# Block-diagonal factor built in head-innermost column order, plain copies of the folded weights, and a new written-out order

## The chip, the cores and the metric

The kernel runs on one core of one Trainium2 chip. The metric is device time in microseconds (us), the median of several runs. One more execution was taken by the hardware profiler; the rows quoted below come from it. Engine names are those of the profile: PE is TensorE (matmuls), PEld its weight loads, DVE is VectorE, ACT is ScalarE, POOL is GpSimd, SP is SyncE, whose queue issues nearly all DMAs.

## What is computed

A transformer block over 2048 tokens of width 512, batch 1. Its conditioning vector gives six vectors (shift, scale and gate, for each of two halves). The first half is linear attention with 32 heads of width 16, whose feature map is a small matrix per head and a softmax of both signs; the second half is a gated MLP of inner width 1376.

```python
h = _layernorm(x) * (1 + ca) + sa
qkv = h @ wqkv                                     # q, k, v: 32 heads of 16
pq = einsum('bhsd,hdf->bhsf', q, w_phi)            # the same for k
phi_q = concatenate([softmax(pq), softmax(-pq)])   # the same for phi_k
kv = einsum('bhsf,bhsd->bhfd', phi_k, v);  z = phi_k.sum(s)
o = (phi_q @ kv) / (phi_q @ z + 1e-6)
x = x + ga * (o @ wo)
h = _layernorm(x) * (1 + cb) + sb
x = x + gb * ((sigmoid(h @ w_gate) * (h @ w_up)) @ w_down)
```

All inputs are bf16. Note that `pq` is linear in `h`: `q` and `w_phi` can be folded into one 512 x 512 matrix per side, and so they are here.

## The kernel before

**Tasks and their order.** The kernel is a graph of 1230 named tasks. Each has a function that issues its instructions, the engines on which it may run with a planner's estimate of its cost in us, what it reads and writes, and the buffers that it uses. The string ORDER lists all tasks in one fixed sequence. A suffix (`@A`, `@D`, `@P`) puts a task on ACT, DVE or POOL; without it the first engine of its list is taken. Each engine executes its own tasks strictly in that sequence, and semaphores hold an instruction until its inputs are there. The position of a task against those of another engine says nothing by itself; its position against the tasks of its own engine, and which buffer slot it gets (there are eight PSUM banks), is what counts. The cost estimates are not read when the kernel is built: they only served to make the order.

**Names of tasks.** The digit or digits after a name are the token tile (128 tokens, 16 tiles), or a group of tiles and a quarter of the width:

- `ld_*` loads through SP: `x0b` tokens of tiles 2 and 3, `x0a` of tiles 0 and 1, `wk0/1` the two halves of the key weights, `wv0` the value weights, `wm00a..wm01b` four parts of the first modulation weights, `wmga` and `wmm2` the later ones (`wmm2` is 1536 KB), `wo`, `wg0`, `wu0`, `wd` the big weights.
- `warm*` matmuls on zeros whose result is not used; 6 in `warm0` and 12 `warm1_i`.
- `bd` (L578, POOL) builds the block-diagonal 128 x 128 matrices of `w_phi`, four of them, from `wp_sb` and a mask.
- `tpw`, `wTc` (L659, L662): key weights transposed on PE and copied to SBUF by ACT; `wqT` the same for the query weights by a DMA transpose.
- `fold1k` and `fold0k` (L677, PE): four 128-column matmuls each, transposed weights times `bd`; side 1 is the key side, side 0 the query side. `foldc1k` and `foldc0k` (L684 on ACT, L686 on DVE) copy the result from PSUM into `wqk_f`.
- `st1`, `rs1`, `nmr1`, `xn1`: LayerNorm of a tile; `tph` (L743) its PE transpose; `hm1_gj` (L750 on ACT, L752 on DVE and POOL) the modulation of quarter j of tile group g, which gives `h1T`. Groups 0 and 1 are tiles 0 and 1, group 2 is tiles 2 and 3, group 3 tiles 4 and 5, and so on. `modc1.h` (L628) and `modc1c h` (L633, L634) compute the vectors that `hm1` needs; `modca`, `modc2` (L614) compute later ones.
- `K`, `V`, `Q` (L816, L820, L870): the three projections of a tile, four 512-column matmuls each (an `a`/`b` pair is two halves). `e` and `qe` (L775, ACT) two exponentials of one PSUM bank; `n` and `qn` (L779, DVE) their sums; `r` the reciprocals; `phi` and `qphi` (L786, L783) the products; `va` (L835) the copy of V. `kv` (L282, PE) accumulates over tiles; `kvn`, `kvz` (L294, L299) end that accumulation in `kvb`.
- Behind `kvb`: `num`, `rd`, `u`, `oT`, `out`, `x1` (attention output), `st2`..`mod` (second LayerNorm), `g`, `tg`, `u`, `hm`, `y`, `fin`, `st` (the MLP and the store).

**Column order.** Within each group of 64 folded columns (4 heads of 16 features) everything behind the fold wants the head index innermost: column = feature x 4 + head. `bd` before has the feature innermost, as `w_phi` has. The order is changed in the copy from PSUM to SBUF:

```python
dst = wqk_f[:, kt_in, side * D:(side + 1) * D].rearrange("p (g f h) -> p g h f", f=DH, h=4)
src = ps[:].rearrange("p (g h f) -> p g h f", f=DH, h=4)
act.copy(dst, src)          # or dve.tensor_copy
```

so the source is read along the row and the destination is written at a step of four elements.

**Stages.** First, to about 16 us: loads, LayerNorm, transposes, the key-side fold. Then K and V of the first tiles and, from about 22 us, the query-side fold, without which no Q can run. From about 33 to 64 us: K, V, Q, exponentials, sums and products of all tiles, with `kv` accumulating. From 64 us on: attention output, second LayerNorm and MLP of each chunk of tiles, with the remaining Q tasks in between.

Of the kernel before, what the change touches and what calls it, by code (L numbers as in the profile page):

```python
# [39 lines left out]
ld_x0b wdz warm0 c1 warm1_0 warm1_1 warm1_2 warm1_3 warm1_4 warm1_5 warm1_6 warm1_7 bd ld_x1a st1_3 st1_2 st1_4 st1_5 ld_x0a ld_wk0 rs1_2 nmr1_2 rs1_3 tpw1  # L40
tpw0 wTc1 ld_x1b st1_1 wTc0 c2 xn1_2 xn1_3@A fold11 ld_wk1 rs1_1@P pmem ld_wm01b ld_wm01a st1_7 c3 ld_x2b foldc11 fold10 tpw3 foldc10 nmr1_3 warm1_8 tpw2
nmr1_1 wTc3 wTc2 modc1.1 st1_0 tph23 ld_wm00a ld_wm00b xn1_1 tph12 tph13 modc1c1 ld_x2a fold13 fold12 tph20 tph22 ld_x3a warm1_9 st1_6 xn1_4 rs1_0@P st1_11
st1_10 hm1_23@A hm1_13@A foldc13 xn1_0 hm1_12@A ld_wv0 wqT3 tph21 warm1_10 rs1_4@P modc1.0 foldc12@D nmr1_4 tph02 hm1_22@A xn1_5 modc1c0 rs1_6@P tph10 hm1_21
hm1_02@A hm1_20@A tph30 tph33 tph32 tph31 tph11 tph00 hm1_10@A st1_9 st1_8 nmr1_6 hm1_11@A hm1_00@A K2a hm1_30@A tph03 K2b tph01 e2.0 xn1_7 xn1_6 K3a hm1_32
hm1_33 hm1_01 K3b rs1_5@P K1a K1b ld_wmga wqT0 wqT1 wqT2 hm1_03 warm1_11 n2.0 tph42 tph41 K0a tph43 K0b e3.0 V2a V2b V1a xn1_10 hm1_42@A hm1_41@A nmr1_5
st1_15 xn1_8 xn1_11 st1_14 hm1_31@A e0.0 rs1_8@P hm1_43 tph40 V1b V3a xT1_11 xT1_10 n0.0 nmr1_8 fold03 fold01 va2 st1_12 fold00 V3b xn1_9 hm1_40 n3.0 e1.0
r0.0@A foldc01 foldc00 va1 foldc03 V5 fold02 foldc02 V0a V0b xn1_14 n1.0 tph52 hm1_52 xn1_15 va0 r3.0@A ld_wmm2 phi0.0 modca.0 tph82 Q1 modca.1 tph53 st1_13
ld_wo hm1_53 Q0 phi3.0@D r2.0@A phi2.0@D Q2 hm1_60@P r1.0@A hm1_82@A modcac hm1_63@P qe0.0 rs1_7@P nmr1_7 phi1.0@D xn1_13 qe1.0 qn0.0 qn1.0 qe2.0 va3 kv0.0
K4a K4b K6a V4 va4 qn2.0 tph51 kv1.0 e4.0 K6b kv2.0 tph50 K5a kv3.0 K5b xT1_13 hm1_62@P xn1_12 xT1_12 qphi0.0@P Q4 qphi0.1 hm1_50@A hm1_51@A V8 K7a e5.0 tph81
qe4.0 va5 K7b va8 hm1_73 V7 pT0 K8 qphi2.1 hm1_61@P qphi2.0@P n4.0 r4.0 tph80 n5.0 hm1_81 qn4.0 V6 phi4.0@D qphi1.0@P qphi1.1@P kv4.0 qphi4.0 hm1_71@P r5.0@A  # L50
va7 e6.0 hm1_80@A K10 tph83 qphi4.1 K9 va6 e7.0 pT2 n6.0 phi5.0 pT1 e8.0 hm1_83 r6.0 gwa n7.0 K14 n8.0 pT4 phi6.0 e9.0 K11 kv5.0 V10 gra ld_wd2 modc2.0 r7.0@A
n9.0 kv6.0 hm1_70@P hm1_72@P phi7.0@D e11.4 r8.0@A e11.6 e11.0 e14.4 phi8.0 modc2.1 modc2c e11.2 r9.0 n11.0 K13 kv7.0 V13 e10.0 e14.0 e13.0 e13.4 n11.4 n11.6
n14.4 n10.0 n11.2 r11.0 kv8.0 K12 phi9.0 V9 wmod_free gwb ld_wu0 ld_wg0 e12.0 K15 V11 r10.0@A va9 va10 va13 r11.6 n14.0 mask4 wo1 phi11.0 r11.4 r14.0 r11.2
n12.0 n13.0 kv9.0 r14.4@A e15.4 phi11.6@D Q6 V12 phi11.4 phi11.2 phi10.0@D e15.0 r12.0@A r13.0@A phi14.4@D phi14.0 Q3 kv10.0 n13.4 n15.4 V15 va11 kv11.0
kv11.2 kv11.4 V14 kv11.6 va12 phi13.0 qe6.0 r13.4 n15.0 r15.4 va15 phi15.4 phi13.4@D va14 Q5 ld_wd r15.0@A phi12.0@D kv12.0 kv13.4 kv14.4 kv13.0 kv15.4 qn6.0
qphi6.0@P qe3.0 phi15.0@D kv14.0 kv15.0 kvz1 kvn1 wo0 wo3 wo2 Q7 qphi6.1@P kvn0 kvz0 qn3.0 num1b num2b num0b num2a num0a qphi3.0@P num1a rd0a rd0b qe5.0 u0a
qe7.0 Q8 u0b grb num4b rd1b wo_all rd2a u1b rd1a rd2b u1a tpo0 oT0 u2b u2a oT2 pT6 qn5.0 Q11 num4a tpo1 oT1 out0 x1_0 qe11.0 out1 rd4a st2_0 x1_1 qphi3.1@P
qe8.0 pT3 Q9 wd0 Q15 Q13 rs2_0 nmr2_0 xn2_0 out2 xnT0 rd4b u4a u4b qn7.0 tsw Q10 mod02 mod03 mod00 x1_2 mod01@A qe15.0 g0.1 tg0.1 g0.8 st2_1 tg0.8 qphi5.1@P
qphi5.0@P u0.8 u0.1 g0.3 hm0.8 num3a hm0.1 g0.9 g0.6 u0.3 qe9.0 rd3a num3b qphi7.1@P qphi7.0@P tg0.3 tg0.9 u3a u0.9 hm0.3 rd3b hm0.9 u0.4 u0.6 u3b qe10.0
tg0.6 rs2_1 nmr2_1 u0.10 g0.4 hm0.6 num6a rd6a tg0.4 oT4 pT5 hm0.4 g0.10 g0.7 tg0.10 tg0.7 g0.0 u0.7 num6b g0.5 u6a xn2_1 hm0.7 hm0.10 tg0.0 qe13.0 tg0.5 wd8  # L60
wd3 wd1 wd5 rd6b u0.0 st2_2 out4 xnT1 mod12@A mod11@A mod10@A mod13@A Q12 oT3 pT7 out3 u0.5 u6b qn11.0 hm0.0 x1_4 g0.2 tg0.2 hm0.5 x1_3 g1.7 g1.5 oT6 u0.2
num7b u1.5 tg1.5 g1.0 wd4 hm0.2 rd7b hm1.5 qphi11.0@P u7b u1.0 u1.7 g1.1 num5b tg1.0 hm1.0 tg1.7 u1.1 hm1.7 st2_3 g1.3 u1.3 qphi11.1@P wd9 pT11 tg1.3 tg1.1
hm1.3 rd5b wd2 g1.4 u1.4 tg1.4 num5a num7a rd7a rd5a hm1.1 u7a out6 u1.6 g1.10 qe12.0 u5b tg1.10 u1.10 y0.0 g1.2 u5a x1_6 hm1.10 u1.2 oT7 rs2_2 nmr2_2 hm1.4
oT5 wd6 g1.6 tg1.6 Q14 y0.1 y0.2 g1.9 xn2_2 hm1.6 qn10.0 st2_4 xn2_3@D st2_6 xnT2 wd10 g1.8 num11a qphi10.0@P wd7 tg1.2 tg1.8 hm1.2 out7 out5 y0.3 tg1.9 x1_5
u1.8 y0.4 y1.0 qphi10.1@P y1.1 st2_5 hm1.8 y1.2 num11b y1.3 y1.4 u1.9 y0.5 y1.5 xnT3 mod22 rd11a y0.6 mod20@A mod21@A hm1.9 u11a rs2_3 pT10 mod23@P x1_7
nmr2_3 y1.6 y1.7 y1.8 y0.7 y1.9 y1.10 rd11b u11b fin1 g2.7 g2.5 u2.7 g2.0 u2.0 st2_7 tg2.5 xn2_5 tg2.7 hm2.7 qn9.0 tg2.0 qe14.0 rs2_4 hm2.0 xn2_4@P u2.5 g2.6
g2.1 tg2.1 nmr2_4 hm2.5 u2.1 hm2.1 g2.4 y0.8 g2.2 tg2.2 y0.9 tg2.4 qphi9.0@P xn2_6 u2.2 u2.4 num10b u2.8 u2.3 xn2_7 xnT5 xnT4 y0.10 g2.3 oT11 qphi9.1 hm2.4
qn8.0 mod32@P tg2.6 hm2.2 tg2.3 qn15.0 mod31@P qphi8.1@P qphi8.0@P qphi15.1@P mod33@P u2.6 y2.0 hm2.3 rd10b fin0 y2.1 y2.2 hm2.6 xnT6 pT9 g2.10 g2.8 tg2.8
tg2.10 out11 xnT7 pT8 mod43@A mod40@P u2.10 num10a g2.9 num9a mod42@A mod41@A x1_11 qphi15.0 y2.3 y2.4 y3.0 y3.1 y3.2 y2.5 u10b hm2.8 rd9a u9a rd10a u10a oT10
hm2.10 num9b rd9b u2.9 qn14.0 mod30@A tg2.9 y3.3 y3.4 y3.5 y3.6 y3.7 hm2.9 g3.0 qn13.0 qn12.0 u9b tg3.0 qphi12.1@P qphi12.0@P pT12 u3.0 hm3.0 g3.8 g3.3 num8a  # L70
tg3.3 rd8a tg3.8 st2_11 y3.8 u3.3 g3.1 u8a hm3.3 bnd3 u3.1 out10 x1_10 y3.9 y2.6 y3.10 y2.7 qphi13.1@P qphi14.1@P qphi14.0 u3.8 hm3.8 g3.7 g3.4 u3.7 y2.8
qphi13.0@P wr st1 tg3.1 bnd1 num12b st0 fin3 hm3.1 pT15 oT9 pT14 st2_10 tg3.7 tg3.4 y2.9 num8b g3.6 rd8b u8b num12a out9 y2.10 fin2 g3.2 u3.4 hm3.7 tg3.2
rs2_6 y4.0 y4.1 u3.2 hm3.4 nmr2_6 x1_9 hm3.2 xn2_10 xn2_11@P tg3.6 u3.6 g3.5 rd12b u12b u3.5 oT8 out8 num14b y7.0 tg3.5 hm3.6 st2_9 hm3.5 rd12a u12a x1_8
st2_8 num15a y5.0 rd15a u15a u3.9 y7.1 y5.1 y7.2 y7.3 num15b pT13 g3.9 rd15b u15b xnT10 st3 xnT11 oT15 st2 rs2_5 nmr2_5 xn2_9@P tg3.9 y7.4 y7.5 y4.2 y7.6 y7.7
hm3.9 rd14b g3.10 y4.3 u3.10 y5.2 xnT9 y5.3 y5.4 num13a mod62@A xn2_8 tg3.10 hm3.10 mod60@A out15 y4.4 y4.5 y7.8 num14a y6.0 xnT8 mod52@A x1_15 oT12 u14b
rd13a num13b y5.5 y5.6 y5.7 y5.8 y5.9 y5.10 fin5 rd13b mod61 y4.6 y6.1 y4.7 y4.8 y7.9 y6.2 out12 mod63 u13a mod50@P bnd2 y7.10 y4.9 u13b fin7 mod51@P mod53@A
u4.0 g4.0 u4.1 tg4.0 rd14a u14a oT14 hm4.0 g4.1 g4.5 tg4.5 u4.9 tg4.1 oT13 g4.2 out14 hm4.1 st2_15 x1_12 u4.5 y4.10 st7 y6.3 g4.8 tg4.8 u4.8 x1_14 hm4.5 bnd0
st2_14 fin4 st4 rs2_8 out13 x1_13 nmr2_8 g4.7 g4.6 tg4.7 g4.9 u4.7 st2_12 hm4.7 tg4.9 hm4.9 hm4.8 st2_13 y6.4 u4.4 y9.0 xn2_14@P xn2_15@P xnT15 xnT14 rs2_7
nmr2_7 y6.5 y6.6 y6.7 y6.8 u4.6 y6.9 u4.2 g4.4 tg4.2 st5 tg4.6 xn2_12@P xnT12 hm4.6 hm4.2 xn2_13@D xnT13 g4.10 u4.3 y8.0 y6.10 g4.3 tg4.4 y10.0 y9.1 mod83@A
tg4.3 mod81@A hm4.4 hm4.3 mod70 bndb y10.1 y8.1 u4.10 y9.2 y10.2 y8.2 y10.3 y8.3 y8.4 y8.5 y8.6 y8.7 y8.8 y11.0 mod71@P y10.4 y10.5 y10.6 y10.7 y10.8 y10.9  # L80
mod73@P tg4.10 mod82@P mod72@P mod80@A fin6 y9.3 y8.9 bndc y11.1 hm4.10 y8.10 y10.10 fin10 st10 fin8 g5.2 y9.4 g5.9 y9.5 y11.2 y9.6 u5.1 y9.7 y11.3 y11.4 y9.8
y9.9 tg5.2 u5.8 u5.2 hm5.2 g5.8 tg5.8 hm5.8 tg5.9 y11.5 y11.6 y9.10 u5.7 u5.0 g5.7 u5.5 st8 tg5.7 bndd hm5.7 st6 g5.3 g5.1 tg5.1 hm5.1 tg5.3 u5.3 g5.6 hm5.3
g5.0 tg5.0 hm5.0 u5.6 u5.9 tg5.6 g5.10 fin9 hm5.6 hm5.9 g5.4 y13.0 y13.1 tg5.4 tg5.10 u5.10 hm5.10 u5.4 y13.2 y11.7 g5.5 y13.3 y11.8 hm5.4 y11.9 y11.10 ldf
# [974 lines left out]
```

## Time and profile before

| what | value |
|---|---|
| median of 3 runs | 210.25 us (210.24 to 210.35) |
| the profiled execution's own time | 210.67 us |
| its span, first to last instruction | 208.8 us |
| around the span in that execution | 1.87 us |
| mean granted PE clock | 0.984 |
| last matmul ends (the last window with PE work) | 205.45 us |

The profiled execution is 0.42 us above the median. A table of windows gives, for each stretch, the us that each engine was busy, the number of instructions in brackets, the granted PE clock as a share of full speed, and the DMA share. A row of the groups gives line, engine, operation, output and inputs with shapes, count, total busy us, mean ns of one, idle time of the engine just ahead of them and what ended it. Instructions of one engine overlap a little at their ends, so group totals sum to more than the engine's busy time.

### The profile page before, as it was taken

The numbers are of one execution on the slowest core, as the hardware profiler recorded it, in microseconds if no ns is written. First come the engines' busy times: TensorE is split into PE (matmuls) and PEld (weight loads), VectorE is DVE, ScalarE is ACT, GpSimd is POOL, SyncE is SP. The second block draws the span as 40 slices with busy tenths as digits, with TensorE's granted clock in tenths as the row PEclk, the third lists the DMA queues.
The fourth block names the chain that finished last, engine by engine and source line by source line (L and its number), as shares of the span: only waits on it lengthen the run. The fifth ranks groups of instructions, "written<-read, shape, count | busy, mean of one in ns | idle before, by whom it ended". The sixth has DMA issues, their size and how long they took to land.

```text
span 208.8 us, 4136 instructions
## 1 busy us (share of the span) xinstructions
PE 198.0 (95%) x1448; PEld 107.7 (52%) x1471; DVE 162.5 (78%) x376; ACT 111.3 (53%) x257; POOL 101.8 (49%) x141
## 2 busy tenths in 40 slices
...
GB/s 179 332 318 182 62 358 81 109 122 56 279 394 167 126 80 102 68 87 53 87 139 28 100 127 85 69 101 25 75 0 72 57 27 25 52 6 25 6 52 79
DMA packets 49453, 22.94 MB, mean 110 GB/s; under 512 B 38065, under 2 KB 47634, under 8 KB 49426
## 3 DMA queue, kind: packets, MB, share of 16 engines
...
q14 instruction: 14, 0.11, 0.2%
q10 hardware_dynamic: 530, 0.02, 0.1%
HBM read 11.58 MB, written 2.10 MB: 66 GB/s over the span
## 4 chain that ended last, share of the span: by engine, by line
PE 70%; ACT 11%; DVE 8%; DMA 8%; issue 1%
PE y_ps L485 18%; PE u_ps L447 16%; PE g_ps L447 16%; DMA wmod_sb<-gdr 6%; PE k_ps L816 4%; PE a_ps L356 4%; ACT wqk_f L684 4%; PE q_ps L870 3%; ACT h1T L750 3%; PE v_ps L820 2%; ACT e L775 2%; DVE qks L779 2%; PE num L326 1%; DVE o L333 1%; DMA x_sb<-in_A_x_dram 1%
## 5 line engine op out<-in xcount | busy, mean ns | idle before, releaser
L457 ACT ACTIVATE tg<-g_ps 128x512 bf16<-128x512 f32 (+4 forms) x66 | 29.2, 456 | 70.3 <-PE g_ps L447 43.8
L468 DVE SCALAR_TENSOR_TENSOR wmod_sb<-tg,u_ps 128x512 bf16<-128x512 bf16 (+4 forms) x63 | 30.5, 492 | 18.6 <-ACT tg L457 12.2
L485 PE MATMUL y_ps<-wd_sb,wmod_sb 128*128 128x512 bf16 (+4 forms) x183 | 44.2, 366 | 0.2
L783 POOL TENSOR_TENSOR qphi<-qe,qks 128x512 bf16<-128x512 bf16 x25 | 26.3, 1070 | 9.2 <-issue 6.1
L447 PEld LDWEIGHTS <-wg_sb 128*128 128x128 bf16 (+1 forms) x252 | 21.6, 99 | 16.0 <-issue 0.4
L447 PEld LDWEIGHTS <-wu_sb 128*128 128x128 bf16 (+1 forms) x252 | 21.6, 99 | 15.7 <-issue 0.2
L485 PEld LDWEIGHTS <-wmod_sb 128*128 128x128 bf16 (+1 forms) x187 | 17.4, 98 | 17.8 <-issue 0.7
L447 PE MATMUL u_ps<-wT_sb,wu_sb 128*128 128x512 bf16 (+2 forms) x123 | 23.9, 322 | 0.1
L447 PE MATMUL g_ps<-wT_sb,wg_sb 128*128 128x512 bf16 (+2 forms) x120 | 23.4, 320 | 0.2
L447 PE MATMUL u_ps<-wqk_sb,wu_sb 128*128 128x256 bf16 (+4 forms) x128 | 19.9, 287 | 0.0
L447 PE MATMUL g_ps<-wqk_sb,wg_sb 128*128 128x128 bf16 (+4 forms) x127 | 19.6, 286 | 0.3
L779 DVE TENSOR_REDUCE qks<-qe 128x64 bf16<-128x1024 bf16 x16 | 19.1, 1207 | 0.4 <-ACT qe L775 0.4
L779 DVE TENSOR_REDUCE ks<-e 128x64 f32<-128x1024 bf16 (+2 forms) x22 | 19.2, 910 | 0.0
L492 DVE TENSOR_TENSOR ot<-y_ps,x 128x512 bf16<-128x512 f32 (+2 forms) x17 | 11.1, 652 | 10.4 <-PE y_ps L485 8.5
L870 PE MATMUL q_ps<-wqk_f,h1T 128*128 128x512 bf16 x62 | 17.3, 407 | 1.5 <-ACT wqk_f L684 1.4
L775 ACT ACTIVATE e<-k_ps 128x512 bf16<-128x512 f32 (+2 forms) x44 | 17.7, 521 | 0.1
L775 ACT ACTIVATE qe<-q_ps 128x512 bf16<-128x512 f32 x32 | 17.1, 612 | 1.0 <-PE q_ps L870 0.9
L786 POOL TENSOR_TENSOR phi<-e,kr 128x1024 bf16<-128x1024 bf16 (+2 forms) x11 | 15.2, 1391 | 4.9 <-ACT h1T L750 2.2
L816 PE MATMUL k_ps<-wqk_f,h1T 128*128 128x512 bf16 x61 | 15.9, 379 | 0.5 <-ACT h1T L750 0.3
L356 PE MATMUL a_ps<-wo_sb,oT 128*128 128x512 bf16 x60 | 15.9, 379 | 0.2
L820 PE MATMUL v_ps<-wv_sb,h1T 128*128 128x512 bf16 x61 | 15.9, 379 | 0.2
L376 POOL TENSOR_SCALAR ve<-mv 128x2 f32<-128x2 f32 (+1 forms) x8 | 1.8, 224 | 28.9 <-DVE mv L366 28.9
...
## 6 DMA issues: line engine op xcount, KB each, us to landing
...
wmod_sb<-in_w_mod_dram SPq DMA_DIRECT2D x1, 1536.0 KB, 7.1
wu_sb<-in_B_w_up_dram SPq DMA_DIRECT2D x1, 1376.0 KB, 7.6
wg_sb<-in_B_w_gate_dram SPq DMA_DIRECT2D x1, 1376.0 KB, 10.6
...
```

The costliest lines, as they stand in the source:

```text
L356: pe.matmul(ap_[:], lhsT=oT[:, j, :], rhs=wo_sb[:, j, :], start=(j == 0), stop=(j == KT - 1))
L447: pe.matmul(ps[:fsz, 0:n], lhsT=w[:, j, ft * P:ft * P + fsz], rhs=h[:, j, 0:n], start=(j == 0), stop=(j == KT - 1))
L457: G.add(f"tg{k}.{ft}", {"ACT": 0.13 + n * 0.00083}, lambda e, tg=tg, g_ps=g_ps, fsz=fsz, n=n: act.activation(tg[:fsz, 0:n], g_ps[:fsz, 0:n ...
L468: dve.scalar_tensor_tensor(hm_all[:fsz, hm[k].slot, ft, 0:n], tg[:fsz, 0:n], 1.0, u_ps[:fsz, 0:n], op0=ALU.add, op1=ALU.mult)
L485: mm = pe.matmul(y[:, 0:c1 - c0], lhsT=hm_all[:fsz, hm[k].slot, ft, tl * P:(tl + 1) * P], rhs=wd_sb[:fsz, ft, c0:c1], start=(ft == 0), sto ...
L775: act.activation(ee[:, a:b, s].rearrange("p g f h -> p g (f h)"), kp[:, a * 64:b * 64].rearrange("p (g n) -> p g n", n=64), ACT.Exp, scale ...
L779: dve.tensor_reduce(ks[:, a:b].rearrange("p g s h -> p (g s) h"), ee[:, a:b].rearrange("p g s f h -> p (g s) h f"), axis=AX.X, op=ALU.add)
L783: engine(e).tensor_tensor(ph[:].rearrange("p (g s f h) -> p g s f h", s=2, f=DH, h=4)[:, :, s], ee[:, :, s], ks[:, :, 1 - s].unsqueeze(2). ...
L786: engine(e).tensor_tensor(ph[:, a * P:b * P].rearrange("p (g f h) -> p g f h", f=DH, h=4), ee[:, a:b].rearrange("p g s f h -> p (g s) f h" ...
L816: pe.matmul(kp[:], lhsT=h1T[:, j, t * P:(t + 1) * P], rhs=wqk_f[:, j, D:2 * D], start=(j == 0), stop=(j == KT - 1))
L820: pe.matmul(vp[:], lhsT=h1T[:, j, t * P:(t + 1) * P], rhs=wv_sb[:, j, :], start=(j == 0), stop=(j == KT - 1))
L870: pe.matmul(qp[:], lhsT=h1T[:, j, t * P:(t + 1) * P], rhs=wqk_f[:, j, 0:D], start=(j == 0), stop=(j == KT - 1))
```

## The change

Three things are changed in one step.

1. `bd` is built with the head innermost, in two POOL instructions of half the width. They read `wp_sb` with each element repeated four times and the mask at a step of 16 elements.
2. The copies of the folded weights take the row as it stands; source and destination are both contiguous.
3. ORDER is replaced as a whole by another sequence of the same 1230 tasks. With it, the engine of 67 tasks changes; all eight `foldc` are on ACT. The task list also gains DVE as a permitted engine for the modulation of groups 6 and 7; no task of the new order uses it.

```diff
-    G.add("bd", {"POOL": 1.15}, lambda e: pool.tensor_tensor(
-        bd[:].rearrange("p k (h f) -> p k h f", f=DH), wp_sb[:].unsqueeze(2).to_broadcast([P, KT, 8, DH]),
-        bm.unsqueeze(1).to_broadcast([P, KT, 8, DH]), op=ALU.mult), w=["bd"])
+    def f_bd(e):
+        for g in range(2):
+            pool.tensor_tensor(bd[:, :, 64 * g:64 * g + 64].rearrange("p k (f h) -> p k f h", h=4), wp_sb[:].unsqueeze(3).to_broadcast([P, KT, DH, 4]),
+                               bm[:, 4 * g:4 * g + 4, 0].unsqueeze(1).unsqueeze(1).to_broadcast([P, KT, DH, 4]), op=ALU.mult)
+    G.add("bd", {"POOL": 1.25}, f_bd, w=["bd"])
...
-                dst = wqk_f[:, kt_in, side * D:(side + 1) * D].rearrange("p (g f h) -> p g h f", f=DH, h=4)
-                src = ps[:].rearrange("p (g h f) -> p g h f", f=DH, h=4)
+                dst = wqk_f[:, kt_in, side * D:(side + 1) * D]
                 if e == "ACT":
-                    act.copy(dst, src)
+                    act.copy(dst, ps[:])
                 else:
-                    dve.tensor_copy(dst, src)
+                    dve.tensor_copy(dst, ps[:])
...
-                w = {"ACT": 0.25 + 0.11 * n, "POOL": 0.12 + 0.165 * n}
+                w = {"ACT": 0.25 + 0.11 * n, "POOL": 0.12 + 0.165 * n, "DVE": 0.14 + 0.065 * n}
```

The head of the new ORDER, up to the first tiles' Q and a little beyond:

```
pmem ld_x0b wdz warm0 c1 warm1_0 warm1_1 bd st1_2 st1_3 warm1_2 warm1_3 c2 rs1_2 ld_x0a ld_wk0 warm1_4 tpw0 st1_0 rs1_0 wTc0 st1_1 ld_wk1 rs1_1 c3 xn1_0
nmr1_1 nmr1_2 ld_x1b st1_6 st1_7 tpw1 tpw3 wTc3 wTc1 tpw2 fold10 foldc10 wTc2 ld_wm00b ld_x1a ld_wm00a tph00 fold11 fold13 rs1_4 foldc13 fold12 foldc12 xn1_3
xn1_2 xn1_1 modc1.0 tph10 tph11 st1_4 tph20 tph01 ld_x2b foldc11 tph22 warm1_5 modc1c0 hm1_11@A nmr1_4 xn1_6 xn1_7 st1_5 rs1_3@P st1_11 st1_10 warm1_6
hm1_20@A hm1_10@A tph21 warm1_7 tph41 tph42 hm1_21 rs1_6@P nmr1_3 tph13 ld_wm01a ld_wm01b modc1.1 hm1_01@A hm1_00@A hm1_41@A tph03 tph23 K2a ld_x2a tph02
modc1c1 st1_8 ld_x3a warm1_8 K1a hm1_23 xn1_5 xn1_4 tph12 nmr1_6 st1_9 hm1_03@A hm1_13@A hm1_02@A ld_wv0 wqT3 xn1_10 xn1_11 rs1_5@P K0a K0b tph31 hm1_42@A
warm1_9 hm1_12@A hm1_22@A tph32 e0.0 K3a tph30 K3b hm1_30@A ld_wmga K1b tph33 warm1_10 tph40 st1_14 st1_15 st1_13 hm1_31@A hm1_32 wqT0 e3.0 wqT1 K2b hm1_40
nmr1_5 rs1_8@P n0.0 nmr1_8 hm1_33 e2.0 V0a V1a fold03 xn1_9 xn1_8 V1b V0b e1.0 n2.0 V2a V2b tph50 hm1_50 warm1_11 xn1_15 xn1_14 n1.0 V3a wqT2 fold00 fold01
tph43 r0.0@A va1 va0 phi0.0 foldc03 fold02 foldc01 foldc02 n3.0 st1_12 foldc00 xT1_10 xT1_11 r2.0 va2@D ld_wmm2 modca.0 modca.1 hm1_60@P hm1_63@P hm1_62@P
tph82 hm1_82@A r3.0@A modcac r1.0@A phi2.0@D phi1.0@D V3b K4a K4b rs1_7@P Q0 Q2 kv0.0 Q1 qe0.0 va3 qe2.0 hm1_43@A qe1.0 modc2.0 tph52 modc2.1 tph51 nmr1_7
xn1_12 xn1_13 phi3.0@D ld_wo qn0.0 modc2c e4.0 kv1.0 qn2.0 hm1_52 kv2.0 Q4 K5a kv3.0 xT1_12 xT1_13 qphi0.0@P
...
```

Of the tasks behind this head, the change moves `modc2.0`, `modc2.1` ahead (in the old order they stand behind `V10` and `K11`), moves `grb` (the broadcast load of the MLP's gate vector) ahead of `ld_wg0` and behind `ld_wd` and `ld_wu0`, and ends in the same tasks as before (`y15`, `fin15b`, `st15b`).

The matching stretch of the old ORDER, per engine: ACT has `rs1_2 rs1_3 wTc1 wTc0 c2 xn1_3 foldc11 foldc10 wTc3 wTc2 modc1c1 hm1_23 hm1_13 foldc13 hm1_12 hm1_22 modc1c0 hm1_02 hm1_20 hm1_10 hm1_11 hm1_00 hm1_30 e2.0 e3.0 hm1_42 hm1_41 hm1_31 e0.0 va2 e1.0 r0.0 foldc01 foldc00 va1 foldc03 foldc02`, with `foldc12` on DVE. SP has `ld_x0b ld_x1a ld_x0a ld_wk0 ld_x1b ld_wk1 ld_wm01b ld_wm01a ld_x2b ld_wm00a ld_wm00b ld_x2a ld_x3a ld_wv0 wqT3 ld_wmga wqT0 wqT1 wqT2 xT1_11 xT1_10 ld_wmm2 ld_wo`.

More of the change, by code (lines that the diff above doesn't have):

```diff
@@ L39 @@
 ORDER = """
[L40 to L83, printed above, removed]
```

41 lines of the change are left out of this document (38 added, 3 removed).

## The prediction

> **What bounds the kernel now.** I read the page first, then a table of windows, then the instruction groups of one stretch.
>
> ```profile
> PE 198.0 (95%) x1448; PEld 107.7 (52%) x1471; DVE 162.5 (78%) x376; ACT 111.3 (53%) x257; POOL 101.8 (49%) x141
> PE 70%; ACT 11%; DVE 8%; DMA 8%; issue 1%
> ```
>
> PE is busy for 95% of the span and holds 70% of the chain that ended last. ACT, 53% busy on average, still holds 11% of that chain, so there is a stretch in which ACT sets the pace. The windows show where (columns: length; busy us of PE, PEld, DVE, ACT, POOL; granted PE clock; DMA share).
>
> ```profile
> 5.33:26.20 20.87, 17.78 (x158) 10.66 (x159) 19.29 (x55) 19.75 (x44) 17.23 (x31) 0.92 1.00 223
> 26.20:34.00 7.80, 6.17 (x42) 3.03 (x43) 4.92 (x11) 6.74 (x17) 4.29 (x7) 0.78 0.70 264
> 34.00:63.70 29.70, 29.22 (x283) 16.37 (x287) 29.20 (x53) 29.15 (x83) 23.11 (x23) 1.00 0.66 188
> 63.70:100.00 36.30, 35.85 (x379) 24.58 (x381) 34.82 (x102) 23.34 (x59) 31.80 (x35) 1.00 0.44 90
> 100.00:205.45 105.45, 104.86 (x579) 51.66 (x588) 71.99 (x154) 31.04 (x58) 23.63 (x35) 1.00 0.28 59
> ```
>
> From 34 us to the last matmul PE loses 0.48 + 0.45 + 0.59 = 1.5 us in 171 us, so a reordering there can win 1.5 us at most. The loss is earlier. From 26.2 to 34 us PE is idle for 7.80 - 6.17 = 1.63 us and has a clock of 0.78, which loses another 0.22 x 7.80 = 1.7 us: **3.3 us together**. What PE waits for there:
>
> ```profile
> PE q_ps L870 <- ACT wqk_f L684: 1.4, 2, 0.9
> DVE h1T L752 <- PE tp_h L743: 2.5, 1, 2.5
> ```
> ```profile
> 26.57 2.41 ACT L684 CAST wqk_f<-fold_ps 128x512 bf16<-128x512 f32 x2
> 30.24 2.34 PE L870 MATMUL q_ps<-wqk_f,h1T 128*128 128x512 bf16 x5
> ```
>
> The first Q waits for the last copies of the query-side fold, which end at 26.57 + 2.41 = 28.98 us; PE runs without gaps only from 30 us on, and DVE stands 2.5 us behind a transpose that is queued on PE behind that Q. ACT is full up to there, and the copies are its largest group. ACT from its first LayerNorm instruction to the first `qe`:
>
> ```profile
> L684 ACT CAST wqk_f<-fold_ps 128x512 bf16<-128x512 f32 x7 | 8.6, 1342 | 0.0
> ...
> L750 ACT ACTIVATE h1T<-tp_h,modc 128x256 bf16<-128x256 bf16 x8 | 4.3, 563 | 0.0
> L750 ACT ACTIVATE h1T<-tp_h,modc 128x128 bf16<-128x128 bf16 x6 | 2.5, 456 | 0.0
> L662 ACT COPY wT_sb<-tp_w 128x512 bf16<-128x512 bf16 x4 | 2.2, 622 | 0.0
> ...
> L726 ACT ACTIVATE xn<-x_sb,nmr,rs 128x512 bf16<-128x512 bf16 x1 | 0.8, 821 | 0.0
> L775 ACT ACTIVATE qe<-q_ps 128x512 bf16<-128x512 f32 x1 | 0.6, 597 | 0.9 <-PE q_ps L870 0.9
> L708 ACT ACTIVATE ve<-mv,eps 128x2 f32<-128x2 f32 x2 | 0.6, 296 | 3.2 <-DVE mv L702 3.2
> L709 ACT ACTIVATE rs<-ve 128x2 f32<-128x2 f32 x2 | 0.4, 204 | 0.1
> ```
>
> The sixteen groups of this answer sum to 29.6 us, in a window of 26.87 us (5.33 to 32.2) of which ACT idled 2.1 us (0.9 of it ahead of the first `qe`): its instructions overlap at their ends, and 24.8 / 29.6 = 0.84 of a row's sum is what it takes of the path.
>
> **The copy.** A strided copy takes 1.34 us on ACT, and
>
> ```profile
> L686 DVE CAST wqk_f<-fold_ps 128x512 bf16<-128x512 f32 x1 | 1.3, 1286 | 0.1
> L835 ACT CAST vaug<-v_ps 128x512 bf16<-128x512 f32 x16 | 9.2, 619 | 0.0
> ```
>
> 1.29 us on DVE, while the same cast of the same bank for V, whose destination has a gap after every 16 elements, takes 0.62 us. No row shows a fully contiguous one; between 0.6 and 1.3 I take 0.62, the row it resembles most (`wT_sb` above gives the same).
>
> **The path on ACT, part by part**, between 5.33 us and the end of the last query-side copy. The two orders hold the same four `e`, four `wTc`, two `modc1c`, two `va` and one `r` there. They differ so:
>
> - copies: seven at 8.6 become eight (the one on DVE comes over) at 0.62: 5.0 - 8.6 = -3.6
> - `rs1`: four instead of two, (0.6 + 0.4) / 2 = 0.5 each: +1.0
> - `xn1_3` goes to POOL: -0.8; the small `c2` (0.2) comes ahead of the stretch: -0.2
> - modulation of 128 columns, eight instead of six: 2 x 0.42 = +0.84; of 256 columns, six instead of seven: -0.54
>
> Together -3.3 us by rows, x 0.84 = **-2.8 us**: the last copy ends at 26.2 instead of 29.0. PE has then done as much as before: in both orders K and V of tiles 0 to 3, both folds, and one more projection (`V5` before, `K4` after). So the stall of 26 to 30 us goes, and the gain stays under the 3.3 us that PE lost there. What is late next is DVE, at its sums.
>
> **DVE.** Rows of DVE up to the end of `kvb`, and its last instruction:
>
> ```profile
> L752 DVE TENSOR_SCALAR h1T<-tp_h,modc 128x256 bf16<-128x256 bf16 x9 | 3.5, 399 | 3.5 <-PE tp_h L743 2.5 <-ACT modc L634 1.0
> L797 DVE RECIPROCAL kr<-ks 128x64 bf16<-128x64 f32 x3 | 1.6, 550 | 0.0
> L361 DVE TENSOR_TENSOR x<-a_ps,x_sb 128x512 f32<-128x512 f32 x16 | 10.8, 681 | 0.4 <-PE a_ps L356 0.2
> 63.49 0.22 DVE L299 SCALAR_TENSOR_TENSOR kvb<-kvacc,mask 128x16 bf16<-128x16 f32 x1
> ```
>
> It is 98% busy from 34 to 63.7 us (29.20 of 29.70), where `kvb` ends and the second half can start, so it must come forward by 2.8 us too. Up to `kvb` the new order takes from it one copy (1.29) and two modulations (0.4 each), and adds a reciprocal (0.55) and a `va` (no row on DVE; at most the 0.68 of a sum read from PSUM, `x1`): 1.29 + 0.8 - 0.55 - 0.68 = 0.9 us of work less. The rest comes from the 2.5 us wait quoted above, which goes with the stall: 3.4 us in all, enough.
>
> **`bd`.** Price and cover:
>
> ```profile
> 5.45 1.15 POOL L578 TENSOR_TENSOR bd<-wp_sb,bmask 128x512 bf16<-128x512 bf16 x1 [2.91 <-DMA wp_sb<-in_A_w_phi_dram]
> 7.91 0.88 PE L677 MATMUL fold_ps<-bd,wT_sb 128*128 128x128 bf16 x8 [0.49 <-ACT wT_sb L662]
> 8.80 0.65 POOL L584 MEMSET vaug<- 128x32 bf16 x4
> 9.04 0.41 POOL L585 MEMSET ones_f<- 128x1 f32 x1
> ...
> L786 POOL TENSOR_TENSOR phi<-e,kr 128x256 bf16<-128x256 bf16 x3 | 1.8, 607 | 0.0
> ```
>
> Two halves at the 0.61 of a POOL product of 256 columns make 1.2 us; slowed by the copies' ratio 1342 / 619 they would make 2.5. I take 1.2. At 5.45 us, where the load of `w_phi` releases it, `bd` then ends between 6.7 and 7.95 us, and its reader was late at 7.91 us by ACT's transposed copy, which is no earlier in the new order (`rs1_0` goes ahead of it): nothing either way up to 2.5 us. Were that cover gone, each us more would hold the key-side fold by as much. `pmem` (0.65 + 0.41 us), now ahead of `bd`, lies in POOL's 2.91 us wait. The Trainium skill, page "GPSIMD Engine Reference", section "Performance pitfalls for Q7 kernels", says that reads at a step of over 8 bytes cost half as much again per element; the mask is read at 32 bytes, so by it an estimate is 1.15 x 1.5 = 1.7 us and the sum does not change; no run shown has such a read.
>
> **Loads and queues.** SP issues the same DMAs. The second key half comes fourth instead of sixth, which can only help the fold. `grb` and `wd` pass `wg0`:
>
> ```profile
> 50.98 0.50 SPq L559 DMA_DIRECT2D wg_sb<-in_B_w_gate_dram  x1
> ...
> wg_sb<-in_B_w_gate_dram SPq DMA_DIRECT2D x1, 1376.0 KB, 10.6
> ```
>
> The gate weights landed at 61.6 us, and are first read behind `kvb` (63.7), the first attention outputs and the second LayerNorm. That hides a few us of delay: nothing, up to about 5 us.
>
> **The added wait.** `modc2.0` moves from 48 us to just behind Q1. It reads `wmm2`:
>
> ```profile
> L712 POOL TENSOR_TENSOR rs<-ve,mhalf 128x2 f32<-128x2 f32 x5 | 3.6, 720 | 0.4
> L711 POOL TENSOR_SCALAR ve<-mv 128x2 f32<-128x2 f32 x5 | 1.1, 227 | 1.3 <-DVE nmr L717 1.3
> ...
> 20.32 1.52 POOL L730 TENSOR_SCALAR xn<-x_sb,rs,nmr 128x512 bf16<-128x512 bf16 x2 [1.00 <-DVE nmr L717]
> 21.87 2.53 SPq L735 DMA_TRANSPOSE h1T<-xn  x2
> 24.44 0.58 SPq L556 DMA_DIRECT2D wmod_sb<-in_w_mod_dram  x1
> 40.67 0.86 PE v_ps L820 x4
> ...
> 48.15 0.81 PE L614 MATMUL modc_ps<-sc_bf,wmod_sb 128*128 128x1 bf16 x24
> wmod_sb<-in_w_mod_dram SPq DMA_DIRECT2D x1, 1536.0 KB, 7.1
> ```
>
> The load is issued behind two transposes that wait for `xn1_11` on POOL. At the old time it lands at 24.44 + 7.1 = 31.5 us. PE reaches `modc2.0` at 26.2 + three Q at 0.86 (the row of a V, as long) + a `kv` of 0.3 = 29.1 us. Behind it on PE stand `modc2.1`, three `kv`, `Q4`, `K5`, and ACT waits for those. In the new order `xn1_11` has three `rs1` fewer ahead of it on POOL (0.72 + 0.23 each by their rows of 2 columns, 2.9 in all): done at 21.84 - 2.9 = 19.0 instead of 21.84, the load issued at 21.6 and landed at 28.7: no wait, by a little, with 0 to 2.4 us as bounds.
>
> **Sum.** -2.8 (copies and what ACT takes over) + 0 (`bd`) + 0 (loads) + 0 (`modc2`) = -2.8. Span 208.8 - 2.8 = 206.0; with the 1.87 us around it 207.9 for an execution like the profiled one, which is 0.42 over the median. **Forecast: 210.25 - 2.8 = 207.4 us** (own range of the case 206.4 to 208.4: an engine's path added by rows is good to about 1 us).
>
> **Rivals.**
> - *More than the copies.* The whole 3.3 us and the 1.5 us that PE loses later: 4.8, that is 205.4. For it: PE's first K moves ahead too. Against: 1.5 us in 171 is near nothing already. Chance 0.12.
> - *DVE paces.* Only its 0.9 us of work comes off, its waits return elsewhere (the new order puts `hm1_23` ahead of its sums, behind a load and ACT): 209.3. For it: 98% busy for 30 us. Chance 0.17.
> - *All of it is given back*, within 0.4 us of 210.25. Chance 0.05.
> - *PE stands at `modc2.0` (the slower one).* With the load at its old time PE waits 31.5 - 29.1 = 2.4 us, and the clock drops as it did after 26.2 us, 1.7 us more: 4.1 - 2.8 = +1.3, 211.5. It decides from a landing after 29.1 + 2.8 - 1.7 = 30.2 us with the drop, 31.9 without. Chance 0.14. The Trainium skill, page "TensorE: Matmul & The Clock Gate", section "Part 1: The HAM clock gate", says that the clock falls to half only after an idle window of about 3.4 us; by that rule the 2.4 us wait costs no clock and this case ends at 207.4 + 2.4 = 209.8, not slower. The trace speaks against so strict a reading: 1.63 us of idle in 7.8 went with 0.78.
> - *The copies stay at 1.3* (the read of PSUM, not the stride, is what costs): eight on ACT make 8 x 8.6 / 7 = 9.8 where 5.0 was taken, 4.8 x 0.84 = 4.1 on the path: -2.8 + 4.1 = +1.3, 211.5. The 0.62 of V's copy speaks against. Chance 0.02.
>
> **Chances and range.** Forecast 0.50, more 0.12, DVE 0.17: faster by over 0.2% (0.42 us, about what a measurement of this kernel can tell from no change) 0.79; same 0.05; slower 0.14 + 0.02 = 0.16. The range 205.3 to 210.9 leaves out the worse half of the slower cases and little else.
>
> **What would show it.** Copies at L684's place near 0.62 us, eight on ACT; the last query-side copy ending near 26 us; PE idle from 26 to 34 us under 0.5 us and a clock near 1.0 there; `kvb` near 61 us instead of 63.5; `bd` as two POOL instructions ending before 8 us; `modc2` without a wait for DMA. Wrong if PE shows a new wait over 1 us behind 26 us, or if `kvb` comes no earlier.

## The result and the profile after

The changed kernel takes 205.31 us (median of 4 runs, 204.49 to 205.61) against 210.3 for the kernel before beside it; the ratio is 0.9748 with a 95% interval of 0.971 to 0.9787. That is 5.0 us faster, where 2.8 was forecast: the sign and the mechanism held, the size did not. Its profiled execution took 205.02 us with a span of 203.3.

The page, and the windows with the same borders as before:

```profile
PE 194.9 (96%) x1447; PEld 106.7 (52%) x1471; DVE 160.6 (79%) x374; ACT 105.9 (52%) x257; POOL 102.1 (50%) x143
PE 75%; DVE 8%; ACT 4%; DMA 4%; issue 4%; POOL 3%; SPq 0%; POOLq 0%; DVEq 0%
```
```profile
5.33:26.20 20.87, 18.76 (x179) 11.26 (x180) 19.79 (x56) 19.91 (x55) 18.11 (x27) 1.00 1.18 274
26.20:34.00 7.80, 7.47 (x109) 4.77 (x109) 7.80 (x14) 7.55 (x22) 5.05 (x8) 1.00 0.54 164
34.00:63.70 29.70, 29.13 (x250) 15.72 (x253) 28.79 (x63) 27.41 (x77) 24.97 (x23) 1.00 0.71 197
```

ACT's share of the chain fell from 11% to 4%. From 26.2 to 34 us PE is busy for 7.47 instead of 6.17 us, at a full clock instead of 0.78: 3.0 of the 3.3 us that it lost there came back. But the stretch ahead of it changed as well: 18.76 instead of 17.78 us busy and a clock of 1.00 instead of 0.92, which is 1.0 + 0.08 x 20.87 = 2.7 us more of PE. The forecast took that stretch as it was.

The copies, the new `bd`, the last query-side copies, the load and the reader that it holds, and the end of `kvb`, from the groups and the timeline of the changed kernel:

```profile
L685 ACT CAST wqk_f<-fold_ps 128x512 bf16<-128x512 f32 x8 | 4.2, 601 | 0.0
L580 POOL TENSOR_TENSOR bd<-wp_sb,bmask 128x256 bf16<-128x256 bf16 x2 | 1.5, 770 | 2.1 <-DMA wp_sb<-in_A_w_phi_dram 2.1
```
```profile
5.24 1.50 POOL L580 TENSOR_TENSOR bd<-wp_sb,bmask 128x256 bf16<-128x256 bf16 x2 [2.13 <-DMA wp_sb<-in_A_w_phi_dram]
7.53 0.40 PE L679 MATMUL fold_ps<-bd,wT_sb 128*128 128x128 bf16 x4
21.41 0.57 SPq L556 DMA_DIRECT2D wmod_sb<-in_w_mod_dram  x1
23.28 2.06 ACT L685 CAST wqk_f<-fold_ps 128x512 bf16<-128x512 f32 x4
28.90 0.82 PE L616 MATMUL modc_ps<-sc_bf,wmod_sb 128*128 128x1 bf16 x24 [0.22 <-DMA wmod_sb<-in_w_mod_dram]
58.37 0.42 DVE L294 TENSOR_TENSOR kvb<-kvacc,mask 128x256 bf16<-128x256 f32 x1
```

A copy takes 0.60 us instead of 1.34. The last one ends at 23.28 + 2.06 = 25.34 us, 3.6 earlier than before (28.98) and 0.9 earlier than forecast. `kvb` ends at 58.79 us instead of 63.71: 4.9 us earlier, 1.3 us more than the last copy, and this is the number that reaches the end.

### The profile page after: what moved, and what is told of

Read it like the earlier page. It is cut to its first block, busy times and chain, and to the rows that moved or that the text cites. A ratio compares the mean times of both kernels' runs of the same rounds, so it can differ in the third digit from the quotient of the medians.

```text
span 203.3 us, 4138 instructions
## 1 busy us (share of the span) xinstructions
PE 194.9 (96%) x1447; PEld 106.7 (52%) x1471; DVE 160.6 (79%) x374; ACT 105.9 (52%) x257; POOL 102.1 (50%) x143
## 4 chain that ended last, share of the span: by engine, by line
PE 75%; DVE 8%; ACT 4%; DMA 4%; issue 4%; POOL 3%; SPq 0%; POOLq 0%; DVEq 0%
PE y_ps L485 19%; PE u_ps L447 18%; PE g_ps L447 17%; PE a_ps L356 5%; DMA wmod_sb<-in_w_mod_dram 4%; PE k_ps L817 3%; PE warm L600 3%; DVE ks L780 3%; PE num L326 2%; POOL phi L787 2%; PE q_ps L871 2%; PE v_ps L821 2%; PE g_ps L449 1%; ACT h1T L751 1%; DVE qks L780 1%
## 5 line engine op out<-in xcount | busy, mean ns | idle before, releaser
L457 ACT ACTIVATE tg<-g_ps 128x512 bf16<-128x512 f32 (+5 forms) x66 | 28.8, 455 | 66.7 <-PE g_ps L447 39.5
L784 POOL TENSOR_TENSOR qphi<-qe,qks 128x512 bf16<-128x512 bf16 x24 | 25.1, 1063 | 3.9 <-DMA pT<-qphi 1.0
L447 PE MATMUL u_ps<-wqk_sb,wu_sb 128*128 128x128 bf16 (+4 forms) x127 | 19.8, 286 | 0.2
L787 POOL TENSOR_TENSOR phi<-e,kr 128x1024 bf16<-128x1024 bf16 (+2 forms) x10 | 14.5, 1454 | 3.9 <-ACT kr L795 2.1
L871 PE MATMUL q_ps<-wqk_f,h1T 128*128 128x512 bf16 x60 | 15.7, 379 | 0.2
```

What stands on the lines that cost most here:

```text
L447: pe.matmul(ps[:fsz, 0:n], lhsT=w[:, j, ft * P:ft * P + fsz], rhs=h[:, j, 0:n], start=(j == 0), stop=(j == KT - 1))
L457: G.add(f"tg{k}.{ft}", {"ACT": 0.13 + n * 0.00083}, lambda e, tg=tg, g_ps=g_ps, fsz=fsz, n=n: act.activation(tg[:fsz, 0:n], g_ps[:fsz, 0:n ...
L784: engine(e).tensor_tensor(ph[:].rearrange("p (g s f h) -> p g s f h", s=2, f=DH, h=4)[:, :, s], ee[:, :, s], ks[:, :, 1 - s].unsqueeze(2). ...
L787: engine(e).tensor_tensor(ph[:, a * P:b * P].rearrange("p (g f h) -> p g f h", f=DH, h=4), ee[:, a:b].rearrange("p g s f h -> p (g s) f h" ...
L871: pe.matmul(qp[:], lhsT=h1T[:, j, t * P:(t + 1) * P], rhs=wqk_f[:, j, 0:D], start=(j == 0), stop=(j == KT - 1))
```

## The experiments

**The change taken apart, and a clock test.** Theory COPY: the length of the copies is the cause. Rival ORDER: the new sequence is. Theory CLOCK: most of the gain is PE's clock, which by this theory falls when PE stands idle. The changed kernel ran again beside them.

> The changed kernel again, on the same chip as the next three. Both theories: 205.3 us, ratio about 0.975 to before. A share of PE clock below 0.995 should go with a time above 205.5, since 0.01 of clock over a stretch of 200 us is about 1 to 2 us.

It took 206.11 us (204.89 to 207.18), ratio 0.9792 (0.9721 to 0.9864). The four executions stand in the order of their clock, 204.89 at 1.0 and 207.18 at 0.983; two at 0.992 are 0.9 us apart, so the clock does not settle the time alone.

The copy alone: the old ORDER, with the two edits of `bd` and of the copy.

> The old order with the new bd and the plain copies. Theory COPY (the length of the copies on ACT's path is the cause, the order only rides on it): ACT saves seven copies of 1.23 against 0.6, 4.3 us by rows, 3.6 on the path; the query-side copies end near 25.4 us instead of 29.0, PE's idle from 26 to 34 us falls below 0.5 us, the clock there is near 1.0, and the time is 206 to 207. Theory ORDER (the new sequence is the cause): a gain under 1 us, 209.3 to 210.3.

205.36 us (205.19 to 205.43), ratio 0.9739 (0.9676 to 0.9803). COPY holds; the whole gain is there without the new order, and more steadily. Its groups and the end of its `kvb`:

```profile
L685 ACT CAST wqk_f<-fold_ps 128x512 bf16<-128x512 f32 x7 | 3.8, 596 | 0.0
L687 DVE CAST wqk_f<-fold_ps 128x512 bf16<-128x512 f32 x1 | 0.7, 686 | 0.0
```
```profile
58.44 0.22 DVE L299 SCALAR_TENSOR_TENSOR kvb<-kvacc,mask 128x16 bf16<-128x16 f32 x1
```

The order alone: the new ORDER, with the old `bd` and strided copies.

> The new order with the old bd and the strided copies, all eight on ACT. Theory COPY: ACT loses 8 x 0.7 = 5.6 us by rows, 4.7 on the path against the changed kernel; 210 or more, as slow as before or slower. Theory ORDER: 206 to 208.

210.42 us (209.97 to 212.06), ratio 0.9976 (0.9933 to 1.0019): the same as before. Its copies and its end of the first half:

```profile
L684 ACT CAST wqk_f<-fold_ps 128x512 bf16<-128x512 f32 x8 | 9.6, 1375 | 0.0
```
```profile
63.74 0.42 DVE L294 TENSOR_TENSOR kvb<-kvacc,mask 128x256 bf16<-128x256 f32 x1
```

The new order has an eighth long copy on ACT and loses nothing by it, so it may be better by about that much; more than that it is not. ORDER falls.

The first clock test adds matmuls on zeros to the kernel before (shown are the settings; the loops that read them are left out):

```diff
+FILL = {8: 3}            # warm1_8: three matmuls instead of one
+FILLF = {(1, 3): 4}      # four ahead of fold13, into its own bank
+FILLQ = {(1, 0): 5, (1, 2): 3}   # around the first Q, adding zeros to its bank
```

> The kernel before with 14 more matmuls on zeros in the places where PE stood idle (2 behind the key-side transposes, 4 ahead of the fold at 11 us, 8 around the first Q); they change no value. Theory CLOCK (more than half of the 5 us is clock that PE got back by being kept busy): clock 0.995 or more, 3 us faster, 207. Rival (the time goes with the wait for the copies, and the clock is a side effect that costs nothing by itself): 210.2, whatever the clock.

210.32 us (209.96 to 210.9) at a clock of 0.998 to 1.0, ratio 0.9986 (0.9957 to 1.0015). On its face CLOCK falls, but the timeline shows a flaw:

```profile
28.13 1.24 PE L877 MATMUL q_ps<-wd_sb 128*128 128x512 bf16 x5 [0.91 <-ACT wqk_f L689]
29.64 0.81 PE L877 MATMUL q_ps<-wd_sb 128*128 128x512 bf16 x3
```

The eight matmuls around Q stand behind the same wait as Q. They did not fill it, they came after it and took 1.7 us of PE. The same without these eight:

> The kernel before with only the six extra matmuls on zeros of its key-side fold (2 behind the key-side transposes, 4 ahead of the fold at 11 us), none around the first Q, because there the eight of the first filled kernel stood behind the same wait as Q and took 1.7 us of PE themselves. Theory BY-PRODUCT (the slow clock falls on time in which PE waits for ACT anyway): the clock rises to 0.992 or more and the time stays within 0.5 us of before, 210.2. Theory CLOCK: each stretch brought back to a full clock is worth 1.7 us, 207 to 208.6.

209.61 us (209.21 to 211.79), ratio 0.9969 (0.9939 to 0.9999), 8 of 11 runs at a clock of 1.0. The medians are 1.1 us apart (209.61 against 210.69 beside it), and the ratio gives 0.7 with an interval of 0.0 to 1.3. So a full clock alone is worth about 1 us to the kernel before, between the two theories. Where it comes from, with the last query-side copies and, last, the first `qe` of the kernel before:

```profile
5.33:26.20 20.87, 17.66 (x161) 10.33 (x162) 19.29 (x56) 19.57 (x44) 16.55 (x31) 1.00 1.00 222
26.20:34.00 7.80, 5.99 (x49) 3.15 (x49) 5.74 (x12) 7.65 (x19) 4.73 (x8) 1.00 0.72 267
```
```profile
26.74 2.42 ACT L689 CAST wqk_f<-fold_ps 128x512 bf16<-128x512 f32 x2
28.08 0.59 PE L879 MATMUL q_ps<-wqk_f,h1T 128*128 128x512 bf16 x2 [0.92 <-ACT wqk_f L689]
30.01 1.89 PE L879 MATMUL q_ps<-wqk_f,h1T 128*128 128x512 bf16 x8
31.35 3.04 ACT L780 ACTIVATE qe<-q_ps 128x512 bf16<-128x512 f32 x6
```
```profile
32.19 2.06 ACT L775 ACTIVATE qe<-q_ps 128x512 bf16<-128x512 f32 x4 [0.91 <-PE q_ps L870]
```

The first Q is no earlier (28.08 against 27.91 us): up to there the slow clock fell on time in which PE waited for ACT. Behind the stall PE is what ACT and DVE wait for, its next eight Q matmuls take 1.89 us (3.04 before), and `qe` follows 0.84 us earlier than before (32.19). From the end of the last copy to the first `qe` it is 31.35 - 29.16 = 2.2 us instead of 32.19 - 28.98 = 3.2.

**Which copies, and which side of the copy.** Theory SUM: each copy on ACT's path costs its own length, on either side. Rival LAST FOLD: only what stands ahead of the first Q through the query side counts. In the kernel with the copy alone, one side's copies are strided again (`if side == 0:` or `if side == 1:` ahead of the old `rearrange`).

> Old order, new bd, the four query-side copies strided and the four key-side ones plain, so that the query features come out in the wrong column order; the amount of work is unchanged. Theory SUM (every copy ahead of the last of them on ACT's path costs the same, whichever side): 4 x 0.75 x 0.84 = 2.5 us over the copy alone, 207.9. Theory LAST FOLD (as predicted: only the stall ahead of the first Q counts, and ACT's work ahead of it is what it waits for through the query side): all of the gain goes, 210.

208.13 us (207.48 to 208.9), ratio 0.9858 (0.9801 to 0.9915): 2.8 us over the copy alone.

> Old order, new bd, the four key-side copies strided (three on ACT, one on DVE) and the query-side ones plain, so that the key features come out in the wrong column order; the amount of work is unchanged. Theory SUM: 3 x 0.75 x 0.84 = 1.9 us from ACT and at most the 0.7 of the one on DVE, 207.3 to 208. Theory LAST FOLD: under 0.5 us, 205.4 to 205.9.

207.54 us (207.31 to 208.41), ratio 0.9846 (0.9791 to 0.9901): 2.2 us over it. SUM holds and LAST FOLD falls, since the copies of both sides cost. A strided copy is 1.31 - 0.60 = 0.71 us longer; four make 2.84 and cost 2.8, and three on ACT make 2.1 and cost 2.2 together with the one on DVE. These times do not tell whether the factor of 0.84 belongs there: each interval reaches 1.2 us to either side, and the copy alone ran on another chip. The traces say more. The last query-side copy, in the copy alone and then with the query side strided:

```profile
23.63 1.10 ACT L685 CAST wqk_f<-fold_ps 128x512 bf16<-128x512 f32 x2
24.89 2.42 ACT L689 CAST wqk_f<-fold_ps 128x512 bf16<-128x512 f32 x2
```

It ends at 24.73 us, then at 27.31, and at 26.63 with the key side strided: 2.6 and 1.9 us later, for 2.7 and 2.1 us more of busy time in the group. That is nearly in full. The two sides add up to 5.0 of the 5.3 us that the copy alone gained.

Which side of the copy is slow: the kernel before with the permutation moved from the write (`wqk_f`, in SBUF) to the read (`ps`, in PSUM).

```diff
-                dst = wqk_f[...].rearrange("p (g f h) -> p g h f", f=DH, h=4)
-                src = ps[:].rearrange("p (g h f) -> p g h f", f=DH, h=4)
+                dst = wqk_f[...].rearrange("p (g f h) -> p g f h", f=DH, h=4)
+                src = ps[:].rearrange("p (g h f) -> p g f h", f=DH, h=4)
```

> The kernel before, old order and old bd, with the copy turned round: it writes the row in sequence and reads PSUM at a step of 16 elements. The result is the same. Theory WRITE (the step of the bf16 destination in SBUF makes a copy 1.3 us): the copies take 0.6 us and the time is that of the copy alone, 205.4. Theory ANY STEP (a step on either side costs): 1.2 us or more per copy, 210.

205.46 us (205.14 to 205.76), ratio 0.9738 (0.9686 to 0.979). WRITE holds:

```profile
L684 ACT CAST wqk_f<-fold_ps 128x512 bf16<-128x512 f32 x7 | 3.8, 596 | 0.0
L686 DVE CAST wqk_f<-fold_ps 128x512 bf16<-128x512 f32 x1 | 0.7, 684 | 0.0
```

Reading PSUM at a step of 16 elements costs neither engine anything against the plain copy (596 and 686 ns); writing bf16 at a step of four costs both about 0.6 to 0.7 us. These two lines do what the change's two edits do, without a new `bd`.

**The cover of `bd`.** The changed kernel with `bd` built three times over (`for g in (0, 1, 0, 1, 0, 1)`).

> The changed kernel with bd built three times over (six POOL instructions of 0.75 us instead of two), so that it ends near 9.7 us instead of 6.7. Theory COVER as predicted (bd is hidden up to 7.95 us, and each us more holds the key-side fold by as much): 1.8 us slower than the changed kernel, 207. Rival (ACT has other work to take first, so that a late fold costs little until about 9 us): under 0.7 us slower, up to 206.

207.33 us (206.55 to 208.56), ratio 0.9818 (0.9754 to 0.9882): 1.2 us over the changed kernel in its second timing, which ran on another chip, and 2.0 over its first. That is nearer to the 1.8 expected than to the rival's 0.7, but the intervals overlap. The profiled execution is the slowest of the six (208.56 us).

```profile
5.55 4.45 POOL L580 TENSOR_TENSOR bd<-wp_sb,bmask 128x256 bf16<-128x256 bf16 x6 [2.45 <-DMA wp_sb<-in_A_w_phi_dram]
```
```profile
10.05 0.59 PE L679 MATMUL fold_ps<-bd,wT_sb 128*128 128x128 bf16 x4 [2.63 <-POOL bd L580]
```

The fold now waits for `bd`, and its first copy starts at 10.67 us instead of 8.75. The cover was real. It ends between 6.7 us, where `bd` held nothing, and 10.0; in the changed kernel the fold starts at 7.53 us, so it probably ends about there, and not at the 7.95 taken.

**Faster still?** The changed kernel with six matmuls on zeros in its key-side fold (`FILLF = {(1, 1): 4, (1, 2): 2}`):

> The changed kernel with six more matmuls on zeros where PE still stood idle in its key-side fold (8 to 10 us); they change no value. Its runs so far went with the clock: 204.5 to 205.0 us at 0.998 to 1.0, 205.6 to 207.2 at 0.983 to 0.992. Theory CLOCK-VARIES (the spread is PE's clock falling in some executions behind that idle time): clock 0.998 or more in every run, median 204.9, spread under 0.6 us. Rival (the spread has another source, the clock only goes along): the spread stays over 1 us at a full clock.

204.96 us (204.13 to 205.64), ratio 0.972 (0.9679 to 0.9761), clock 0.998 or more. The spread stays at 1.5 us with a full clock, so the rival holds for it: it has another source as well, which stays open.

The new order with the old `bd`, the strided read and the same filling:

> The new order with the old single bd, the copy reading PSUM at a step and writing in sequence, and the six extra matmuls on zeros of the filled kernel. bd was hidden at 1.5 us, so both theories of the copy give the time of the filled changed kernel: 204.5 to 205.2, clock 0.998 or more. If the step in PSUM cost ACT anything, 8 x 0.1 = 0.8 us more.

205.05 us (204.86 to 205.33), ratio 0.9721 (0.9673 to 0.9769). As expected, and steadier; its eight copies take 601 ns each, so the step in the read costs nothing here either. No interval sets any of these versions apart from the changed kernel.

One more task off ACT, in the kernel with the copy alone:

> The copy-alone kernel (old order) with one LayerNorm task of 0.8 us, xn1_3, moved from ACT to POOL, ahead of all its key-side copies. Theory ACT PATH (ACT is still what the first half waits for, us for us): 0.7 faster than copy alone, 204.7. Rival NEXT BOUND (with the short copies DVE and POOL are as full as ACT, and a us off ACT is worth little): 205.2 to 206.

205.65 us (205.4 to 205.79), ratio 0.9742 (0.9678 to 0.9805): no gain. NEXT BOUND holds:

```profile
5.33:26.20 20.87, 19.11 (x186) 11.40 (x184) 20.27 (x57) 19.06 (x51) 18.90 (x35) 1.00 1.03 245
26.20:34.00 7.80, 7.80 (x68) 4.20 (x67) 7.66 (x14) 7.71 (x19) 6.70 (x9) 1.00 0.74 239
```

ACT now idles for 1.8 us of the first row (1.3 in the copy alone), but DVE is busy for 20.27 of 20.87. The first key-side copy starts 0.6 us earlier (8.70 instead of 9.27) and the last query-side one ends no earlier (24.78, 24.73). A us off ACT was worth nearly a us in the kernel before and is worth nothing here. That it is DVE which now sets the pace is read from its busy time and not shown; the task went to POOL, and that may also have cost something.

**One number for all of them.** What is left after `kvb` is the same to about 1 us in every profiled execution. Nine of them:

| kernel | `kvb` ends, us | span, us | difference |
|---|---|---|---|
| before | 63.7 | 208.8 | 145.1 |
| order alone | 64.2 | 208.6 | 144.4 |
| before, key-side filled | 62.6 | 207.9 | 145.3 |
| three times `bd` | 62.2 | 206.8 | 144.6 |
| query side strided | 61.9 | 206.9 | 145.0 |
| key side strided | 60.6 | 205.9 | 145.3 |
| changed kernel | 58.8 | 203.3 | 144.5 |
| copy alone | 58.7 | 203.6 | 144.9 |
| changed, filled | 58.0 | 202.4 | 144.4 |

`kvb` moves by 6.2 us over these kernels, the rest by under 1; the five profiles that are not listed have 144.4 to 145.4 us. The new order shows in the rest: 144.4 to 144.7 us with it, 144.9 to 145.4 with the old one, about 0.5 us that the medians are too rough to show.

## Why the prediction was wrong in size

- **The copy: right.** 0.62 us was taken, 0.60 measured, and the stretch from 26 to 30 us in which Q waited is gone, as forecast. That the gain comes from the copies is shown: copy alone gives all of it, order alone none.
- **The path on ACT: the copies' own term was too small, the first step that failed.** "Seven at 8.6 become eight at 0.62: 5.0" sets a group's busy total, from which overlaps are already taken out, against a count times a mean, from which they are not. Like with like, 8.6 becomes 4.2 (the group's row above): -4.4, not -3.6, and the rows give -4.4 + 0.3 = -4.1 instead of -3.3. The factor of 0.84 for overlap was a smaller fault. The last copy came 3.6 us earlier, 0.89 of 4.1; in the copy alone it came 28.98 - 24.73 = 4.3 us earlier for 8.6 - 3.8 = 4.8 us less of busy time, 0.89 again; in the query-side run it came 2.6 us later for 6.5 - 3.8 = 2.7. So the term measured -3.6 where -2.8 was taken, 0.8 us of the 2.2 by which the forecast was short.

```profile
L689 ACT CAST wqk_f<-fold_ps 128x512 bf16<-128x512 f32 x7 | 6.5, 1024 | 0.0
```

- **What lies behind the last copy: put at nothing, the second step that failed.** PE "has then done as much as before", and the gain "stays under the 3.3 us that PE lost there". But PE recovered 3.0 us in that stretch and 2.7 in the one ahead of it, and `kvb` came 1.3 us more ahead than the last copy did. Idle time of the engine at the end of a chain is where a delay shows, not a bound on what its removal is worth. From the end of the last copy to the first `qe` the kernel before takes 3.2 us, the copy alone 26.98 - 24.73 = 2.25, the changed kernel 26.73 - 25.34 = 1.4. The copy alone, then the changed kernel:

```profile
26.98 3.05 ACT L776 ACTIVATE qe<-q_ps 128x512 bf16<-128x512 f32 x6
```
```profile
26.73 1.08 ACT L776 ACTIVATE qe<-q_ps 128x512 bf16<-128x512 f32 x2
```

- **The clock: missing from the sum, and part of that second step.** It stood in the reading of the bound and in a rival, but not as a term. With the long copies but a full clock (before, key-side filled) the same stretch takes 2.2 us, as in the copy alone: 1.0 of the 3.2 us was clock. The time agrees: about 1 us (0 to 1.3 by the interval) of the 1.7 + 1.7 = 3.4 that the two windows suggest; the rest fell on waiting. In the copy alone all four executions had a clock of 0.999 or 1.0, so in that order the lost clock was part of what the long copies cost; `kvb` came 63.71 - 58.66 = 5.05 us earlier there, 0.8 more than the last copy, and the clock can account for all of that. The changed kernel still fell to 0.983 in one execution, so long copies are not all that it takes.
- **DVE: right as the next engine, and mis-sized.** "3.4 us in all, enough" was used as a condition, when it is the number that carries: the end of `kvb` moved by 4.9. Ahead of it DVE was busy for 53.5 us instead of 55.4, 1.9 less and not 0.9, mainly because the new order also leaves one query-side sum for later; and its waits shrank by 3.0. The kernel before, then the changed one, DVE up to the end of `kvb`:

```profile
L779 DVE TENSOR_REDUCE qks<-qe 128x64 bf16<-128x1024 bf16 x6 | 7.1, 1212 | 0.4 <-ACT qe L775 0.4
```
```profile
L780 DVE TENSOR_REDUCE qks<-qe 128x64 bf16<-128x1024 bf16 x5 | 6.0, 1208 | 0.0
L753 DVE TENSOR_SCALAR h1T<-tp_h,modc 128x256 bf16<-128x256 bf16 x9 | 3.5, 393 | 0.6 <-PE tp_h L744 0.6
```

  The wait for a PE transpose fell from 2.5 to 0.6 us. How the 1.3 us behind the last copy divide between the clock and this lighter DVE in the changed kernel was not separated.
- **`bd`: price low, cover right.** 1.50 us, between the 1.2 taken and the estimate of 1.7 by the page "GPSIMD Engine Reference" of the Trainium skill; it ended at 6.74 us and held nothing, and 1.2 to 2.0 us came of another 3.3. Its reader started at 7.53 us, 0.4 earlier than before, where the forecast had it no earlier.
- **`modc2`: right, narrowly.** The load was issued at 21.41 us (21.6 forecast); PE stood 0.22 us for it at 28.9. The slower rival did not occur.
- **The range** ended at 205.3, the forecast's own part of it at 206.4, and the rival "more than the copies" stood at 205.4 with a chance of 0.12; the time measured is that rival's. Its number fits by luck, since its way did not come: of its 1.5 us behind 34 us at most 0.6 was won, behind `kvb` (145.1 against 144.5 in the table above).
